# An attention and feed-forward kernel: eight more attention slots, spread over two feed-forward halves

## The chip, the cores and the metric

The kernel runs on one core of a Trainium2 chip. The metric is the device time of one execution in microseconds (us), as the median of several runs. Engines carry the profile's names: PE is the matrix engine and PEld its weight loads, DVE the vector engine, ACT the scalar engine, POOL GpSimd, and SP the engine that issues most DMAs.

## The reference

Causal attention with a decay bias, over 8 batches, 8 heads, 576 positions and 64 numbers a head, and behind it a feed-forward block on all 4608 tokens (512 to 2048 to 512, with a piecewise quadratic activation):

```python
scores = scale * np.matmul(q, k.transpose(0, 1, 3, 2))
cum = np.cumsum(np.maximum(s, 0.0), axis=-1)
bias = -(cum[:, :, :, None] - cum[:, :, None, :])
scores = np.where(causal, -1e9, scores + np.minimum(bias, 0.0))
attn = np.exp(scores - np.max(scores, axis=-1, keepdims=True))
attn = attn / (np.sum(attn, axis=-1, keepdims=True) + 1e-09)
x = np.matmul(attn, v)                  # heads laid side by side: tokens x 512
h = x @ w_in
g = np.where(h >= 1, h, np.where(h <= -1, 0.0, (h + 1) ** 2 / 4))
return g @ w_out
```

## The kernel before

**Attention jobs.** Two heads make a pair, so there are 32 pairs n (four to a batch b), and the 576 positions are cut into two halves: hf 0 holds positions 0 to 319 and hf 1 the other 256. A pair and a half make one of 64 jobs, in the order: for each batch, hf 0 of its four pairs, then hf 1 of its four pairs. A job is written as eight slots (`att_slot(j, k)`, k from 0 to 7). Slot 0 prepares the operands (`att_prep`: ACT casts Q1 in L325, K1 in L334 and Q2 in L335, DVE finishes Q1 in L336 and K2 in L339; each of these four tiles has one buffer, so the casts wait until the last scores of the job before are done). Slots 2 to 7 compute one unit of scores each: two PE matmuls (L384 with Q1 and K1, L385 with Q2 and K2) into a PSUM tile s, a minimum on DVE (L390), the exponential on ACT (L401). When both heads of a row block are there, `weights_t` scales them and splits them into pb (L422 to L425, L428), and a transposing DMA brings pb to pt (L429). Slot 7 also does `att_out` of the job before: the matmuls px from pt and vt (L447), and from px the feed-forward's input x (ACT in L458, DVE in L459). The tiles s and px share a ring of two PSUM buffers.

**Feed-forward halves.** Each batch and half is a feed-forward half of 16 steps (ft). Step ft computes a tile h from all four pairs of x (L501, 12 matmuls; the three of the last pair, kt 3, come last), then u and g on ACT, DVE and POOL (L513, L516, L517, L527, L528), and two steps later adds to four tiles y (L540, 12 matmuls). So a half is 384 matmuls, of 320 columns in hf 0 and of 256 in hf 1, and it needs the px of its batch's four jobs of the same hf. Its results leave through o (L554).

**The order.** One loop writes both down, job slots and feed-forward steps in turn. It has 512 rounds j. From round 32 on, a feed-forward half takes 32 rounds (step j // 2, h in even rounds and y in odd ones), and a round takes one attention slot, ahead of its feed-forward matmuls. In rounds 0 to 31, which hold the first half in an order of its own, every fourth round takes two slots:

```python
for _ in range(1 if j >= 2 * NFT else 1 + (j % 4 == 3)):
    att_slot(t // 8, t % 8)
    t += 1
```

The counter t starts at 32, as the first four jobs lie ahead of the loop. So feed-forward half number q starts, from q = 1 on, after slot 32q + 39, and slot 32q + 39 is the one that writes the px of the last job which that half needs. All 512 slots and the last px are written by round 480 of 512. The order in the source is a priority: the scheduler that builds the program places each instruction on its engine by that priority and by when it expects the inputs. On each engine, instructions then run strictly in the order placed.

Of the kernel before, what the change touches and what calls it, by code (L numbers as in the profile page):

```python
# [25 lines left out]
NFT = DFF // P  # L26
# [47 lines left out]
def attention_ffn(ctx: ExitStack, tc: tile.TileContext, qT, kT, vT, s, w_in, w_out, yT):  # L74
# [194 lines left out]
    def batch_scales(b):  # L269
        m = msc[b]  # L270
        h = hsc[b] = ap.tile([P, 1], F32, tag="hs", name=f"hs{b}")
        V.tensor_scalar(h, m, a_in, 2.0 ** -27, ALU.mult, ALU.mult)

        r = rsc[b] = ap.tile([P, 1], F32, tag="r", name=f"r{b}")
        i = r.bitcast(I32)
        V.tensor_scalar(r, m, a_in, 2048.0, ALU.mult, ALU.mult)
        V.tensor_scalar(r, r, 1.0, None, ALU.max)
        V.reciprocal(r, r)
        V.tensor_scalar(r, r, 2.0 ** 14, None, ALU.mult)
        V.tensor_scalar(i, i, 23, None, ALU.logical_shift_right)  # L280
        V.tensor_scalar(i, i, 127, None, ALU.add)
        V.tensor_scalar(i, i, 1, 23, ALU.logical_shift_right, ALU.logical_shift_left)

        u = usc[b] = ap.tile([P, 1], F32, tag="us", name=f"us{b}")
        V.tensor_scalar(u, h, r, None, ALU.mult)
        w = wsc[b] = ap.tile([P, 1], F32, tag="ws", name=f"ws{b}")
        V.tensor_scalar(w, u, 2.0, None, ALU.mult)
        c = ubi[b] = ap.tile([P, 1], F32, tag="ub", name=f"ub{b}")
        V.tensor_scalar(c, r, 0.5, None, ALU.mult)
        g = gsc[b] = ap.tile([P, 1], F32, tag="gb", name=f"gb{b}")  # L290
        V.reciprocal(g, r)
        V.tensor_scalar(g, g, g, 2.0 ** 14, ALU.mult, ALU.mult)

    def batch_y(b, groups=(0, 1)):
        ysc.setdefault(b, {})
        for i in groups:
            y = ysc[b][i] = ap.tile([P, 1], F32, tag=f"ys{i}", name=f"ys{b}_{i}")
            V.tensor_scalar(y, gsc[b], b_out[i], 2.0 ** -28, ALU.mult, ALU.mult)
# [168 lines left out]
    def att_slot(j, k):  # L467

        if j < len(jobs):
            n, hf = jobs[j]  # L470
            if k == 0:
                att_prep(n, hf)
            if k == 1 and hf == 0:
                v_prep(n)
            if k == V_K and hf == 0:
                v_turn(n)
            if k >= 2:
                scores(n, *UNITS[hf][k - 2])
            if k == 3 and j + 1 < len(jobs):
                att_load(*jobs[j + 1])  # L480
            if k == 1 and j % (2 * NPAIR) == V_J and j // (2 * NPAIR) + 1 < B:
                load_v(j // (2 * NPAIR) + 1)
            if k == 5 and j + 1 < len(jobs) and jobs[j + 1][0] % NPAIR == 0 and jobs[j + 1][1] == 0:
                with tc.issue_after(ttr[0]):
                    batch_start(jobs[j + 1][0] // NPAIR)
        if k == OUT_K and 1 <= j <= len(jobs) and j != NPAIR:
            while j == len(jobs) and late:
                late.pop(0)()
            att_out(*jobs[j - 1])
# [33 lines left out]
    def g_split(first=None):  # L523
        while to_split:
            g, u = to_split.pop()
            with tc.issue_after(first) if first is not None else ExitStack():
                A.copy(g[:, 0], u)  # L527
            G.tensor_tensor(g[:, 1], u, g[:, 0], ALU.subtract)  # L528
# [3 lines left out]
    def ffn_y(b, hf, ft, g, ms=tuple(range(NKT))):  # L532
        h_off, N, _ = HALF[hf]
        if ft == 0:
            for m in ms:
                ys[b, hf, m] = ps_y.tile([P, 512], F32, tag=f"y{m}", name=f"y{b}_{hf}_{m}")
        for m in ms:
            c0 = ft % 2 * 2 * P + m % 2 * P
            for n, (wl, gl) in enumerate(((0, 0), (1, 0), (0, 1))):
                T.matmul(  # L540
                    ys[b, hf, m][:, :N], WO[8 * (m // 2) + ft // 2][:, wl, c0:c0 + P], g[:, gl],
                    start=(ft == 0 and n == 0), stop=(ft == NFT - 1 and n == 2),
                )
        if ft == NFT - 1:
            last = (b, hf) == (B - 1, len(HALF) - 1)
            for m in ms:
                tag, bufs = ("u", 4) if last and m >= 2 else ("o", O_BUFS)
                o = gp.tile([P, N], F32, tag=tag, bufs=bufs, name=f"o{b}_{hf}_{m}")
                y = ys[b, hf, m][:, :N]
                with tc.high_priority(offset=FFN_LEAD):  # L550
                    if last and m % 2:
                        V.tensor_scalar(o, y, ysc[b][m // 2], None, ALU.mult)
                    else:
                        A.activation(o, y, AF.Copy, scale=ysc[b][m // 2])  # L554
                (nc.sync if last and m % 2 else nc.scalar).dma_start(
                    yT[m * P:(m + 1) * P, b * S + h_off:b * S + h_off + N], o
                )

    def ffn_step(s, k):

        b, hf, ft = s // (2 * NFT), s // NFT % 2, s % NFT
        if k == 0:
            ffn_q.append((b, hf, ft, ffn_h(b, hf, ft)))
        elif len(ffn_q) > Y_LAG:
            ffn_y(*ffn_q.pop(0))
# [39 lines left out]
    for j in range(16 * NP):  # L605
        if j % 64 == 48 and j // 64 + 1 < B:
            batch_scales(j // 64 + 1)
            batch_y(j // 64 + 1)
        for _ in range(1 if j >= 2 * NFT else 1 + (j % 4 == 3)):
            att_slot(t // 8, t % 8)  # L610
            t += 1
        with tc.high_priority(offset=W2_LEAD):
            for _ in range(W2_RATE):
                next(tasks, None)
        if j >= 2 * NFT:
            ffn_step(j // 2, j % 2)
        elif j < NFT:
            ffn_step(j, 0)
        else:
            if j == NFT:  # L620
                with tc.high_priority(offset=FFN_LEAD):
                    g_split()
            m = 2 * (j // 8 % 2)
            for i in range(j % 8 * 2, j % 8 * 2 + 2):
                ffn_y(*ffn_q[i], ms=(m, m + 1))
            if j == 2 * NFT - 1:
                del ffn_q[:NFT]
# [32 lines left out]
```

## Time and profile before

| | before |
|---|---|
| times of three runs | 1170.36, 1171.36 and 1180.07 us (median 1171.36) |
| profiled execution | 1178.29 us |
| its span, first to last instruction | 1176.2 us |
| granted PE clock, mean over the span | 0.967 |
| busy share of the span | PE 86%, PEld 66%, DVE 76%, ACT 63%, POOL 59% |
| DMA moved | 158.04 MB, mean 134 GB/s |

The profiled execution is one run, 0.6% above the median. Its share of busy time is an average over three stages: some 92 us ahead of the first feed-forward matmul, the long stage in which attention and feed-forward are mixed, and a last stretch with feed-forward work alone. The granted clock is 1.00 in most of the span and lower in a few places.

### The profile page before, as it was taken

The page shows a single profiled execution, that of the slowest core. Times are in us where ns is not written, and L with a number is a line of the kernel's source. Part 1 is how long each engine was busy: PE and PEld are TensorE (multiplying, and loading weights), DVE is VectorE, ACT ScalarE, POOL GpSimd, SP SyncE. Part 2 cuts the span into 40 slices and gives each one's busy share as a digit, 9 for nine tenths or more (in the row PEclk, how much of TensorE's full clock was granted, in tenths as well). Part 3 has the DMA queues.
Part 4 walks back from the last instruction along what each step waited for, and adds up shares of the span by engine and source line. Part 5 has one row for each costly group of instructions (what it writes and reads, how often), then busy time and mean ns, then how long its engine had stood idle before and what let it go on. Part 6 is the DMA issues. An engine that isn't in the chain of part 4 may idle for free.

```text
span 1176.2 us, 25135 instructions
## 1 busy us (share of the span) xinstructions
PE 1009.5 (86%) x8470; PEld 776.6 (66%) x8470; DVE 892.6 (76%) x2404; ACT 746.0 (63%) x1719; POOL 691.0 (59%) x1169
## 2 busy tenths in 40 slices
PE   0234678699999999799998999899989999899998
PEld 0122345487767867587767867677768867686787
DVE  6879998778777877768777777778778877787633
ACT  4656677567656765767557665667557764777533
POOL 3876268676556664656546654656557564675522
PEclk9997999799998999999999999899999999899999
DMA  8885536867637773776638672876547753767310
GB/s 243 206 195 138 165 85 145 159 139 153 130 73 180 147 148 74 166 139 144 131 84 168 152 149 65 173 142 156 119 98 172 153 133 75 163 132 157 74 34 19
DMA packets 343081, 158.04 MB, mean 134 GB/s; under 512 B 291112, under 2 KB 324264, under 8 KB 342952
## 3 DMA queue, kind: packets, MB, share of 16 engines
q1 hardware_dynamic: 333248, 146.50, 59.0%
q10 hardware_dynamic: 9704, 9.93, 2.7%
q8 instruction: 67, 1.10, 0.4%
q14 instruction: 62, 0.51, 0.1%
HBM read 75.33 MB, written 9.73 MB: 72 GB/s over the span
## 4 chain that ended last, share of the span: by engine, by line
PE 42%; DVE 8%; DMA 5%; POOL 5%; issue 3%; ACT 1%; DVEq 0%; ACTq 0%; POOLq 0%
PE y L540 18%; PE h L501 17%; DMA pt<-pb 4%; PE px L447 3%; POOL pb L422 2%; DVE pb L428 2%; PE s L384 2%; PE s L385 2%; DMA vt<-vb 2%; POOL pb L425 1%; DVE p L390 1%; DVE K L339 1%; DVE h L516 1%; DVE Q L336 1%; POOL vb L350 1%
## 5 line engine op out<-in xcount | busy, mean ns | idle before, releaser
L501 PE MATMUL h<-x,WI 128*128 128x256 f16 (+1 forms) x3072 | 453.0, 292 | 23.4 <-DVE u L517 21.0
L540 PE MATMUL y<-g,WO 128*128 128x256 f16 (+1 forms) x3072 | 453.2, 291 | 17.3 <-POOL g L528 7.4
L501 PEld LDWEIGHTS <-WI 128*128 128x128 f16 x3072 | 292.3, 100 | 118.2 <-issue 28.2
L540 PEld LDWEIGHTS <-WO 128*128 128x128 f16 x3072 | 287.1, 99 | 108.7 <-issue 19.3
L528 POOL TENSOR_TENSOR g<-u,g 128x320 f16<-128x320 f32 (+1 forms) x256 | 199.2, 778 | 209.1 <-ACT g L527 203.9
L513 ACT ACTIVATE u<-h,ub,us 128x320 f32<-128x320 f32 (+1 forms) x256 | 149.3, 584 | 171.8 <-PE h L501 146.7
L401 ACT ACTIVATE p<-p,mn 64x64 f32<-64x64 f32 (+4 forms) x320 | 178.8, 559 | 113.6 <-DVE mn L390 96.4
L516 DVE SCALAR_TENSOR_TENSOR h<-h,ws,u 128x320 f32<-128x320 f32 (+1 forms) x256 | 133.0, 520 | 118.4 <-ACT u L513 117.9
L422 POOL TENSOR_SCALAR pb<-p,rs 64x128 f16<-64x128 f32 (+4 forms) x160 | 113.7, 711 | 152.2 <-DVE rs L418 118.6
L384 PE MATMUL s<-K,Q 128*128 128x288 f32 (+4 forms) x384 | 150.9, 395 | 43.8 <-DVE mn L390 33.3
L428 DVE SCALAR_TENSOR_TENSOR pb<-p,rs,pb 64x128 f16<-64x128 f32 (+4 forms) x160 | 135.8, 849 | 52.0 <-POOL pb L422 51.6
L425 POOL TENSOR_TENSOR pb<-p,pb 64x128 f16<-64x128 f32 (+4 forms) x160 | 165.0, 1032 | 9.2
L390 DVE CUSTOM_DVE_ANT_0 p<-s,mask 64x64 f32<-64x64 f32 (+4 forms) x320 | 134.8, 422 | 41.1 <-PE s L385 36.7
L517 DVE SCALAR_TENSOR_TENSOR u<-u,r,h 128x320 f32<-128x320 f32 (+1 forms) x256 | 130.2, 510 | 7.5
L423 ACT ACTIVATE p<-p,rs 64x64 f32<-64x64 f32 (+4 forms) x160 | 89.3, 559 | 67.2 <-DVE rs L418 60.6
L385 PE MATMUL s<-K,Q 68*128 68x288 f32 (+4 forms) x384 | 121.8, 319 | 9.8 <-ACT p L423 5.5
L447 PE MATMUL px<-pt,vt 128*64 128x256 f16 (+3 forms) x1536 | 87.7, 260 | 38.0 <-DMA pt<-pb 21.8
L384 PEld LDWEIGHTS s<-K,Q 128*128 128x128 f32 (+1 forms) x384 | 74.3, 194 | 68.2 <-DVE mn L390 42.4
L527 ACT CAST g<-u 128x320 f16<-128x320 f32 (+1 forms) x256 | 108.1, 422 | 10.6 <-DVE u L517 10.6
L447 PEld LDWEIGHTS <-vt 128*64 128x64 f16 x1536 | 73.2, 113 | 61.5 <-issue 40.3
L424 POOL TENSOR_SCALAR pb<-p 64x128 f16<-64x128 f32 (+4 forms) x160 | 90.9, 569 | 6.0 <-ACT p L423 2.9
L385 PEld LDWEIGHTS s<-K,Q 68*128 68x128 f32 (+1 forms) x384 | 75.8, 198 | 12.2 <-ACT p L423 5.9
(116 smaller groups left out, 961.4 us busy)
## 6 DMA issues: line engine op xcount, KB each, us to landing
rk<-in_k_dram SPq DMA_DIRECT2D x64, 288.0 KB
rq<-in_q_dram SPq DMA_DIRECT2D x64, 160.0 KB
rk<-in_k_dram SPq DMA_DIRECT2D x64, 160.0 KB
v<-in_v_dram SPq DMA_DIRECT2D x32, 288.0 KB
wir<-in_moe_w_in_dram SPq DMA_DIRECT2D x16, 512.0 KB
rq<-in_q_dram SPq DMA_DIRECT2D x64, 128.0 KB
wor<-in_moe_w_out_dram SPq DMA_DIRECT2D x16, 512.0 KB
out_dram<-o ACTq DMA_DIRECT2D x32, 160.0 KB
```

The lines of the kernel that those rows point to most:

```text
L384: T.matmul(sc[:R, :c1 - c0], Q1[:, hd, qo:qo + R], K1[:, hd, c0:c1], start=True, stop=False)
L385: T.matmul(sc[:R, :c1 - c0], Q2[:KC, hd, qo:qo + R], K2[:KC, hd, c0:c1], start=False, stop=True)
L390: ttr[0] = V.tensor_tensor_reduce(out=Pt[:R, c0:c1], in0=sc[:R, :c1 - c0], in1=mask[:R, mo:mo + c1 - c0], scale=1.0, scalar=3.0e38 if mn i ...
L401: A.activation(Pt[:R, :W], Pt[:R, :W], AF.Exp, bias=m2[:R], scale=-1.0, accum_out=sums[n, i][:R, hd:hd + 1])
L425: G.tensor_tensor(los[1], pw, his[1], ALU.subtract)
L428: V.scalar_tensor_tensor(los[0], pv, rs[:R, :1], his[0], ALU.mult, ALU.subtract)
L447: T.matmul(px[hd * D:(hd + 1) * D, lo:N], VT[:, vl * NB + j, hd * D:(hd + 1) * D], PT[:, 4 * j + 2 * hd + pl, lo:], start=(m == 0), stop=( ...
L501: T.matmul(h[:, :N], WI[4 * kt + ft // 4][:, wl, ft % 4 * P:(ft % 4 + 1) * P], x[:, kt, xl], start=(n == 0), stop=(n == 3 * NKT - 1),)
L513: first = A.activation(u, h[:, :N], AF.Relu, bias=ubi[b], scale=usc[b]).ins
L516: V.scalar_tensor_tensor(h[:, :N], h[:, :N], wsc[b], u, ALU.mult, ALU.max)
L528: G.tensor_tensor(g[:, 1], u, g[:, 0], ALU.subtract)
L540: T.matmul(ys[b, hf, m][:, :N], WO[8 * (m // 2) + ft // 2][:, wl, c0:c0 + P], g[:, gl], start=(ft == 0 and n == 0), stop=(ft == NFT - 1 an ...
```

## The change

```diff
-        for _ in range(1 if j >= 2 * NFT else 1 + (j % 4 == 3)):
+        for _ in range(1 + (j % 4 == 3 if j < 2 * NFT else j % 8 == 3 and j < 6 * NFT)):
             att_slot(t // 8, t % 8)
             t += 1
```

NFT is 16. Rounds 0 to 31 are as before. In rounds 32 to 95 (the halves q = 1 and q = 2) every eighth round, from round 35 to round 91, takes a second slot: eight more. From round 96 on each slot stands eight rounds earlier beside the feed-forward than before, and the last slot is written by round 472. No instruction is added or taken away.

What that makes of the order on the engines, at the place where half hf 1 of batch 6 (q = 13) starts. On PE, px27_1 is the last px that this half needs (pair 27 is the last of batch 6), s28 and s29 are scores of the next jobs, h6_1_0 and h6_1_1 are the first two steps of the half, and y6_0_0 to y6_0_3 are the outputs of the half before. First the rows around the start of px27_1, before:

```order
L384 MATMUL s28_2_0_0_14171<-K1_90,Q1_89 128x320
L385 MATMUL s28_2_0_0_14171<-K2_92,Q2_91 128x320
L384 MATMUL s28_2_1_0_14200<-K1_90,Q1_89 128x320
L385 MATMUL s28_2_1_0_14200<-K2_92,Q2_91 128x320
L447 LDWEIGHTS vt27_12908
L447 MATMUL px27_1_14214<-pt27_1_13815,vt27_12908 64x256
```

And the rows ahead of the start of px27_1 in the changed kernel:

```order
L540 LDWEIGHTS WO15_139
L540 MATMUL y6_0_2_13514<-g6_0_12_14154,WO15_139 128x320
L540 LDWEIGHTS WO15_139
L540 MATMUL y6_0_3_13515<-g6_0_12_14154,WO15_139 128x320
L540 LDWEIGHTS WO15_139
L540 MATMUL y6_0_3_13515<-g6_0_12_14154,WO15_139 128x320
L447 LDWEIGHTS vt27_12760
L447 MATMUL px27_1_14089<-pt27_1_13690,vt27_12760 64x256
```

Before, px27_1 stood right behind the scores s28_2_1_0. Now 13 feed-forward matmuls (5 of h6_1_0 and 8 of y6_0) stand between them. From the last scores of px27_1's own job (s27_4_1_288) to px27_1 there were 58 feed-forward matmuls (40 of 320 columns and 18 of 256) and are now 93 (84 and 9); the scores and the other px in between are the same. For px28_1, the first hf 1 job of the next batch, the same count goes from 70 (42 and 28) to 104 (28 and 76).

Then the rows on PE behind the end of px27_1, before:

```order
L447 MATMUL px27_1_14214<-pt27_1_13815,vt27_12908 64x64
L384 MATMUL s29_0_0_0_14304<-K1_90,Q1_89 64x64
L385 MATMUL s29_0_0_0_14304<-K2_92,Q2_91 64x64
L501 LDWEIGHTS WI12_120
L501 MATMUL h6_1_0_14266<-x6_1_13487,WI12_120 128x256
L501 LDWEIGHTS WI12_120
L501 MATMUL h6_1_1_14312<-x6_1_13487,WI12_120 128x256
```

And in the changed kernel:

```order
L447 MATMUL px27_1_14089<-pt27_1_13690,vt27_12760 64x64
L384 MATMUL s29_0_0_0_14179<-K1_90,Q1_89 64x64
L540 LDWEIGHTS WO7_131
L540 MATMUL y6_0_0_13512<-g6_0_12_14154,WO7_131 128x320
L540 LDWEIGHTS WO7_131
L540 MATMUL y6_0_1_13513<-g6_0_12_14154,WO7_131 128x320
L385 MATMUL s29_0_0_0_14179<-K2_92,Q2_91 64x64
L540 LDWEIGHTS WO15_139
L540 MATMUL y6_0_2_13514<-g6_0_12_14154,WO15_139 128x320
L540 LDWEIGHTS WO15_139
L540 MATMUL y6_0_3_13515<-g6_0_12_14154,WO15_139 128x320
L501 LDWEIGHTS WI0_108
```

WI12 holds the weights of kt 3, so the first h matmul behind px27_1 was one that reads the x made from it. Now 13 others come first: four of y6_0 and the nine of h6_1_1 that read the three earlier pairs. Counted in feed-forward matmuls, px27_1 stood 6 behind the start of its half and stands 7 ahead of it; for the last px of an hf 0 half, 18 ahead become 63.

The third place is the preparation of job (30, hf 1), a little later, on ACT. Before:

```order
L325 ACTIVATE Q1_89<-rq30_1_15350 128x2x256
L332 DMA Q2_91<-cumd_106 2x2x256
L401 ACTIVATE p29_4_1_15431,sm29_4_15380<-p29_4_1_15431,mn29_4_1_288_15460 128x576
L333 DMA K2_92<-cumd_106 2x2x576
L334 CAST K1_90<-rk30_1_15351 128x1152
```

And in the changed kernel:

```order
L325 ACTIVATE Q1_89<-rq30_1_15225 128x2x256
L334 CAST K1_90<-rk30_1_15226 128x1152
L332 DMA Q2_91<-cumd_106 2x2x256
L333 DMA K2_92<-cumd_106 2x2x576
L554 ACTIVATE o6_1_0_15480<-y6_1_0_14550,ys6_0_12888 128x256
```

The cast of K1 now follows the cast of Q1 at once. On PE the distance that it has to cover shrinks: from the last scores of one job to the first scores of the next there stand, besides one px, 18 feed-forward matmuls in place of 25 for job (29, hf 1), 9 in place of 48 for (30, hf 1), and 10 in place of 36 for (31, hf 1).

## The prediction

> **What bounds the kernel now.** I read the page first, then stretches of the span, then PE's waits, and at last single rows at one of the places where PE waits.
>
> ```profile
> span 1176.2 us, 25135 instructions
> PE 1009.5 (86%) x8470; PEld 776.6 (66%) x8470; DVE 892.6 (76%) x2404; ACT 746.0 (63%) x1719; POOL 691.0 (59%) x1169
> PE   0234678699999999799998999899989999899998
> PEclk9997999799998999999999999899999999899999
> ```
>
> PE is the busiest engine, and from the eighth of 40 slices on it is at 9 tenths or nearly. Some slices of PE hold an 8 or a 7, and after the start PEclk falls in much the same places. So the mixed stage is bound by PE, except at places that recur. The stretches at six of these places, with one between two of them and one of the last stretch:
>
> ```profile
> core 0: us, PE busy (x) PEld busy (x) DVE busy (x) ACT busy (x) POOL busy (x), PEclk, DMA share, GB/s
> 352.00:365.00 13.00, 10.31 (x78) 7.80 (x77) 10.01 (x30) 9.13 (x25) 9.16 (x22) 0.74 0.92 209
> 482.00:504.00 22.00, 16.90 (x140) 13.04 (x136) 13.85 (x39) 14.58 (x39) 14.76 (x31) 0.84 0.86 192
> 614.00:635.00 21.00, 16.13 (x150) 13.07 (x151) 14.99 (x40) 15.46 (x42) 14.65 (x31) 0.92 1.00 181
> 744.00:765.00 21.00, 18.06 (x155) 14.31 (x156) 15.70 (x41) 15.54 (x42) 14.36 (x31) 0.84 0.89 181
> 876.00:892.00 16.00, 13.45 (x121) 10.12 (x122) 11.96 (x35) 11.90 (x35) 11.72 (x27) 0.89 0.97 208
> 1003.00:1016.00 13.00, 9.93 (x72) 7.41 (x73) 10.13 (x30) 10.31 (x28) 9.60 (x21) 0.74 0.89 162
> 1016.00:1072.00 56.00, 55.07 (x513) 45.97 (x510) 44.23 (x126) 39.42 (x102) 35.22 (x70) 1.00 0.67 145
> 1140.00:1170.00 30.00, 30.00 (x277) 26.89 (x276) 11.12 (x24) 9.44 (x22) 7.88 (x12) 1.00 0.01 1
> ```
>
> The last number but two is the granted clock. The places lie about 130 us apart ((1003 - 352) / 5), which is one batch, and each is where a half hf 1 starts. There the clock is 0.74 to 0.92, and in between 1.00, with PE busy 55.07 of 56 us. Clock lost is width times (1 - clock): 3.4, 3.5, 1.7, 3.4, 1.8 and 3.4 us. The last row gives the price of a feed-forward matmul where nothing is waited for: 30 us / 277 = 0.108 us at 256 columns, and I take 0.135 us (5/4 of it) at 320. What PE waits for, from the second of these places to the last px:
>
> ```profile
> engine line waited for: us in total, times, longest us
> PE px L447 <- DMA pt<-pb: 14.5, 11, 2.1
> PE s L384 <- DVE mn L390: 8.9, 10, 1.4
> PE y L540 <- POOL g L528: 7.1, 5, 2.6
> PE s L385 <- ACT p L423: 5.5, 5, 1.1
> PE px L447 <- DVE pb L428: 1.8, 1, 1.8
> ```
>
> Only waits of some length are listed; the first line is px waiting for the transposed weights, 11 times. One place in order of time on PE, where half q = 13 starts:
>
> ```profile
> 1001.75 0.42 PE L384 MATMUL s<-K,Q 128*128 128x320 f32 x1 [0.42 <-DVE mn L390]
> 1002.01 0.31 PE L385 MATMUL s<-K,Q 68*128 68x320 f32 x1
> 1003.70 1.51 PE L447 MATMUL px<-pt,vt 128*64 128x256 f16 x30 [1.38 <-DMA pt<-pb]
> 1005.14 0.24 PE L384 MATMUL s<-K,Q 128*64 128x64 f32 x1
> 1006.47 0.21 PE L385 MATMUL s<-K,Q 68*64 68x64 f32 x1 [1.09 <-ACT p L423]
> 1006.53 0.89 PE L501 MATMUL h<-x,WI 128*128 128x256 f16 x6
> ...
> 1009.08 0.53 PE L384 MATMUL s<-K,Q 128*128 128x192 f32 x1 [1.29 <-DVE mn L390]
> ...
> 1010.21 0.49 PE L540 MATMUL y<-g,WO 128*128 128x320 f16 x1
> ```
>
> From 1001.75 to 1010.21 there are only six h matmuls of feed-forward. The rest is a chain of the attention, with four waits: 0.42 + 1.38 + 1.09 + 1.29 = 4.2 us. The half cannot go on, since the x of its last pair is not there, and the matmuls ahead of it in PE's order are used up. The wait of 1.09 is put down to ACT, but L385 reads K2, and DVE ends that just ahead (1005.05 + 1.32), as it ends x at 1006.77:
>
> ```profile
> 1005.05 1.32 DVE L339 TENSOR_TENSOR K<-rk,K 64x640 fp32r<-64x640 f32 x1
> 1006.30 0.47 DVE L459 SCALAR_TENSOR_TENSOR x<-px,ex,x 128x256 f16<-128x256 f32 x1
> ```
>
> That the row of L385 reads 5.5 us in 5 times says that five such places are alike.
>
> **The change, part by part.** It removes and adds no instruction; it puts feed-forward matmuls where PE waited.
>
> *px at the start of hf 1.* From the last scores of its own job to px27_1 there was feed-forward work of 40 x 0.135 + 18 x 0.108 = 7.3 us, and there is 84 x 0.135 + 9 x 0.108 = 12.3 us now. 5.0 us more cover a wait of 1.38 us, and the 0.42 us ahead of it: both go. *K2 of the next job:* between s28_2_1_0 and its use in L385 come 10 matmuls at 0.135 and 5 at 0.108, 1.9 us, against waits of 1.38 + 1.09 = 2.5 us in the same interval; 0.6 us stay. *x:* from the end of px (1003.70 + 1.51) to the end of x it took 1.56 us, and 4 x 0.135 + 9 x 0.108 = 1.5 us now stand there where nothing stood: it just fits. *The scores behind it* (1.29 us): four h matmuls now stand ahead of s29_1_1_0, 0.4 us; 0.9 us stay. So 1.5 us of 4.2 us stay, and 2.7 us go, at five places (q = 5 to 13): **13.5 us**.
>
> *The clock at these five places.* It falls only where PE has such waits; what was lost is 3.5 + 1.7 + 3.4 + 1.8 + 3.4 = 13.8 us. Bounds are 0 and 13.8. With a third of the waits left I take three quarters: **10 us**. In the Trainium skill, "TensorE: Matmul & The Clock Gate", Part 1 and the table "Why this matters for your kernels" say that the clock halves after an idle window of about 3.4 us, and that gaps over about 3 us are to be avoided. The trace does not agree with a reading of that by single gaps, as no wait above is longer than 2.6 us; by that reading these stretches have another cause and this term would be 0.
>
> *px of the first hf 1 job* of each batch:
>
> ```profile
> 1070.45 0.29 PE L385 MATMUL s<-K,Q 68*128 68x288 f32 x1
> 1070.59 0.99 PE L540 MATMUL y<-g,WO 128*128 128x320 f16 x6
> 1072.80 0.41 PE L447 MATMUL px<-pt,vt 128*64 128x256 f16 x4 [1.21 <-DMA pt<-pb]
> ...
> 1056.00:1076.00 20.00, 18.68 (x163) 14.18 (x163) 16.52 (x41) 15.27 (x35) 11.93 (x19) 1.00 0.65 143
> ```
>
> Its feed-forward cover goes from 42 x 0.135 + 28 x 0.108 = 8.7 us to 28 x 0.135 + 76 x 0.108 = 12.0 us: 3.3 us more, against 1.21 us. Of the 14.5 us in the list, 5 x 1.4 are at the starts of hf 1; the other 7.5 and the 1.8 for pb are of this kind. I count **8 us**.
>
> *y waiting for g* (7.1 us in 5 times) comes from POOL and ACT being full of attention work around these places. Nothing in the order bounds it well: between 0 and 7.1 us; halfway, **3.5 us**. *The place at 352*, where only part of the lead is there: px gets cover, x none. Its clock cost 3.4 us and a px wait as at the others is 1.4 us; between 0 and some 7 us, taken: **2.5 us**.
>
> *The eight added slots* are one job. A batch takes 130 us, and its feed-forward 384 x (0.108 + 0.135) = 93 us, so a job costs PE up to (130 - 93) / 8 = 4.6 us. It moves from the last mixed rounds, where PE is full, to halves q = 1 and 2, where PE is nearly full as well: the sum is 0, with 4.6 us either way as the ends.
>
> *What is late next: the operands.* Behind px, less now stands between two jobs' scores. What the casts took, for jobs (29, hf 1) and (30, hf 1):
>
> ```profile
> 1059.10 0.30 PE L385 MATMUL s<-K,Q 68*128 68x288 f32 x1
> 1059.96 1.14 ACT L334 CAST K<-rk 128x1152 fp32r<-128x1152 f32 x1
> 1074.89 1.14 ACT L334 CAST K<-rk 128x1152 fp32r<-128x1152 f32 x1
> ```
>
> K1 is ready 1.7 us after the last scores (1059.40 to 1061.10) in the one, and 5.3 us (1070.74 to 1076.03) in the other. The cover falls to 9 or 10 matmuls, 1.1 to 1.3 us, and a px of up to 1.51 us: some 2.7 us. In the other case ACT had an exponential and an o between, because there was time; now K1 stands right behind Q1, which gives the 1.7 us. The ends are 0 and (5.3 - 2.7) = 2.6 us at three jobs in each of six batches, 47 us; nearest to the row with the same order on ACT, I take 0.7 us a batch: **4 us lost**. DMA moves the same bytes; SP issues the same transfers, moved along with their slots.
>
> The sum: 13.5 + 10 + 8 + 3.5 + 2.5 - 4 = 33.5 us. From the profiled execution's 1178.3 us that is 1144.8 us. It lies 6.9 us above the median of the runs, so I forecast 1171.4 - 33.5 = **1138 us**.
>
> **The rivals.** *The clock stays low at these places*, because the waits that are left are enough for it, or because it has another cause: 10 us less gain, 1148 us. For it: the clock falls where the longest single wait is 1.38 us. Against it: around 1072.80 a lone wait of 1.21 us leaves it at 1.00 (the last row above), so it is several waits close together that go with it. It is also the case that the gap rule of the Trainium skill's page on the clock gate would give. *The lead is not what the name says:* in feed-forward matmuls px27_1 moves by 13, not by the 96 that eight rounds hold, since the scheduler already placed attention by readiness. Then only the px waits go, 5 x 1.4 + 8 = 15 us, with 1 for the place at 352: 1155 us. Against it: px is not the only one with new cover. *No change:* waits move to other places, PE's order being as full as before: 1165 to 1175 us. *Slower:* the casts of the operands, as above. If K1 and Q1 end 5.3 us behind the last scores as they did at 1076.03, the 47 us are lost and 37.5 won, and each such wait of 2.6 us is as long as those that lowered the clock; with 1.7 us more (1.7 to 3.5 were lost at a place) at half of the 18, the time is 1171.4 + 9.5 + 15 = 1196 us. It decides from about 4.8 us: 18 x (4.8 - 2.7) = 37.8 us. The row that speaks against it is the cast at 1061.10. *More:* all bounds at the good end, 5 x 4.2 + 13.8 + 9.3 + 7.1 + 7 = 58 us, 1113 us.
>
> **How the numbers follow.** The forecast (1128 to 1146) gets 0.55, the clock 0.12, the short lead 0.12, more than forecast (1113 to 1128) 0.08, no change 0.08, slower 0.05. A measurement of this kernel can tell about 1% from no change, so faster means below 1159.7 us: 0.55 + 0.12 + 0.12 + 0.08 = 0.87; within 1% 0.08; slower 0.05. The range from 1120 to 1158 us leaves out the two last and about half of "more", some 0.17.
>
> **What would show it.** In the profile after: px waiting for pt falls from 11 times to three or fewer in the mixed stage; in each place where hf 1 starts y or h rows stand between s and px, and PE's clock there is 0.95 or more; L385 behind ACT p falls to 0.6 us a place; PE busy in these stretches is above 9 tenths. It would be wrong if L384 waits for Q or K more than 1 us a job (the casts), if the stretches of low clock stay in number, or if halves q = 1 and 2 take more than 5 us longer than the end wins back.

## The result: 3.4% less time, and the profile after

The changed kernel takes 1132.37 us (median of 4 runs, 1130.65 to 1136.65) where the kernel before takes 1170.92 us (4 runs on the same chip). The ratio measured over these runs is 0.9658, with a 95% interval from 0.9603 to 0.9714 (the two medians alone give 0.9671). The forecast was 1138 us, a gain of 33.5 us; the measured gain is 38.5 us. The profiled execution took 1131.28 us.

The same four lines of the page, now of the changed kernel:

```profile
span 1129.5 us, 25197 instructions
PE 988.2 (87%) x8470; PEld 770.9 (68%) x8470; DVE 879.3 (78%) x2404; ACT 740.2 (66%) x1719; POOL 682.4 (60%) x1169
PE   0234667799999999989998999999999999999998
PEclk9997899789999999999999999999999999999999
```

The work is the same (8470 matmuls; the 62 instructions more are semaphore events, that is, engines waiting for each other), but PE and its clock are at 9 tenths in nearly every slice from the ninth on. The stretches where the halves hf 1 start (q = 3 to 13), and one between:

```profile
341.00:355.00 14.00, 12.14 (x99) 8.97 (x97) 11.20 (x38) 9.63 (x30) 9.21 (x23) 0.88 0.91 187
470.00:490.00 20.00, 17.81 (x156) 14.51 (x152) 14.46 (x49) 14.69 (x43) 13.55 (x32) 0.91 0.85 181
595.00:611.00 16.00, 14.15 (x131) 11.79 (x131) 12.74 (x43) 13.44 (x40) 10.76 (x26) 1.00 0.96 203
717.00:733.00 16.00, 14.01 (x146) 11.73 (x140) 12.50 (x43) 13.01 (x39) 10.71 (x26) 1.00 1.04 214
838.00:854.00 16.00, 14.60 (x150) 12.24 (x147) 12.77 (x44) 13.53 (x39) 11.28 (x27) 1.00 1.02 216
961.00:977.00 16.00, 13.99 (x148) 11.82 (x143) 13.45 (x43) 13.20 (x38) 11.20 (x26) 1.00 0.77 178
977.00:1030.00 53.00, 52.19 (x493) 43.63 (x491) 42.82 (x115) 38.55 (x94) 33.84 (x66) 1.00 0.72 151
```

The clock lost there is 14 x 0.12 + 20 x 0.09 = 3.5 us; before it was 17.2 us. What PE waits for in the mixed stage, by the same view and over the same stretch as before:

```profile
PE s L384 <- DVE Q L336: 6.8, 6, 1.7
PE y L540 <- POOL g L528: 4.3, 5, 1.0
PE s L384 <- DVE mn L390: 3.8, 5, 1.0
PE px L447 <- DMA K<-cumd: 1.9, 2, 1.1
PE y L540 <- ACT g L527: 1.1, 5, 0.2
```

The first line of before (px waiting for pt, 14.5 us) is gone, as is L385 waiting behind ACT p. (Ahead of this stretch, at the place where q = 3 starts, one wait of 0.4 us for pt and one of 1.2 us behind ACT p are left.) A new line leads: scores waiting for Q from L336. The place where q = 13 starts, on PE:

```profile
958.74 0.31 PE L385 MATMUL s<-K,Q 68*128 68x320 f32 x1
958.89 0.72 PE L501 MATMUL h<-x,WI 128*128 128x256 f16 x5
959.45 1.25 PE L540 MATMUL y<-g,WO 128*128 128x320 f16 x8
960.63 1.51 PE L447 MATMUL px<-pt,vt 128*64 128x256 f16 x30
...
962.81 1.36 PE L501 MATMUL h<-x,WI 128*128 128x256 f16 x11
...
965.04 0.33 PE L384 MATMUL s<-K,Q 128*128 128x192 f32 x1 [0.78 <-DVE mn L390]
...
966.71 0.97 PE L540 MATMUL y<-g,WO 128*128 128x320 f16 x6 [0.22 <-ACT g L527]
```

The 13 feed-forward matmuls stand ahead of px, px starts without a wait, and 1.0 us of waiting is left of 4.2 us. At the four other places from q = 5 on, 0.5 to 1.4 us is left, counted in the same way.

In numbers, from the first h of half q = 3 to the end of the span: 831.7 us before (344.5 to 1176.2), 788.7 us after (340.8 to 1129.5), so 43.0 us less. All listed waits of PE from 340 us on fall from 44.2 to 20.4 us (23.8), the time at half clock from 34.1 to 6.8 us (half of the 27.3 us is 13.7), and a job of 4.6 us (an estimate) has gone to the halves before: 42.1 us. The two profiled executions differ by 47 us and the medians by 38.5 us, because the profiled run of before was one of its slower ones (its runs spread from 1170.4 to 1180.1); the split is that of the traces, its sum a little large.

### The profile page after: what moved, and what is told of

Its sections match the earlier page's. It is cut to its first block, busy times and chain, and to the rows that moved or that the text cites. A ratio compares the mean times of both kernels' runs of the same rounds, so it can differ in the third digit from the quotient of the medians.

```text
span 1129.5 us, 25197 instructions
## 1 busy us (share of the span) xinstructions
PE 988.2 (87%) x8470; PEld 770.9 (68%) x8470; DVE 879.3 (78%) x2404; ACT 740.2 (66%) x1719; POOL 682.4 (60%) x1169
## 4 chain that ended last, share of the span: by engine, by line
PE 58%; DVE 16%; POOL 7%; DMA 7%; issue 6%; ACT 5%; ACTq 0%; DVEq 0%; SPq 0%; POOLq 0%
PE y L540 24%; PE h L501 24%; PE px L447 4%; PE s L384 3%; PE s L385 3%; DVE pb L428 3%; DMA pt<-pb 3%; DVE p L390 2%; DVE Q L336 2%; POOL pb L422 2%; DVE h L516 1%; ACT p L401 1%; ACT u L513 1%; DMA wor<-in_moe_w_out_dram 1%; DVE u L517 1%
## 5 line engine op out<-in xcount | busy, mean ns | idle before, releaser
L501 PE MATMUL h<-x,WI 128*128 128x256 f16 (+1 forms) x3072 | 465.1, 291 | 25.6 <-DVE u L517 21.8
L528 POOL TENSOR_TENSOR g<-u,g 128x320 f16<-128x320 f32 (+1 forms) x256 | 203.9, 796 | 163.7 <-ACT g L527 162.8
L422 POOL TENSOR_SCALAR pb<-p,rs 64x128 f16<-64x128 f32 (+4 forms) x160 | 96.9, 606 | 163.1 <-DVE rs L418 111.1
L384 PE MATMUL s<-K,Q 128*128 128x288 f32 (+4 forms) x384 | 148.5, 388 | 44.5 <-DVE mn L390 25.1
L425 POOL TENSOR_TENSOR pb<-p,pb 64x128 f16<-64x128 f32 (+4 forms) x160 | 169.4, 1059 | 9.6
L385 PE MATMUL s<-K,Q 68*128 68x288 f32 (+4 forms) x384 | 121.3, 318 | 4.8 <-POOL K L339 3.6
L384 PEld LDWEIGHTS s<-K,Q 128*128 128x128 f32 (+1 forms) x384 | 73.2, 191 | 67.3 <-DVE mn L390 30.9
L447 PE MATMUL px<-pt,vt 128*64 128x256 f16 (+3 forms) x1536 | 82.8, 259 | 21.0 <-DVE mn L390 6.1
L424 POOL TENSOR_SCALAR pb<-p 64x128 f16<-64x128 f32 (+4 forms) x160 | 94.1, 588 | 10.6 <-ACT p L423 9.4
L385 PEld LDWEIGHTS s<-K,Q 68*128 68x128 f32 (+1 forms) x384 | 74.5, 195 | 8.0 <-POOL K L339 4.1
```

The lines of the kernel that those rows point to most:

```text
L384: T.matmul(sc[:R, :c1 - c0], Q1[:, hd, qo:qo + R], K1[:, hd, c0:c1], start=True, stop=False)
L385: T.matmul(sc[:R, :c1 - c0], Q2[:KC, hd, qo:qo + R], K2[:KC, hd, c0:c1], start=False, stop=True)
L425: G.tensor_tensor(los[1], pw, his[1], ALU.subtract)
L447: T.matmul(px[hd * D:(hd + 1) * D, lo:N], VT[:, vl * NB + j, hd * D:(hd + 1) * D], PT[:, 4 * j + 2 * hd + pl, lo:], start=(m == 0), stop=( ...
L501: T.matmul(h[:, :N], WI[4 * kt + ft // 4][:, wl, ft % 4 * P:(ft % 4 + 1) * P], x[:, kt, xl], start=(n == 0), stop=(n == 3 * NKT - 1),)
```

## The experiments

Theory: PE waited where a half hf 1 starts, because the chain px, x, operands and scores had no feed-forward work beside it; the change puts such work there, and the clock, which falls where PE has little to do, stays up with it. Rivals: the gain is the lead itself, counted in slots; it is made where the slots are added; the clock has a cause of its own. Each kernel's ratio is to the kernel before on the same chip; that kernel's median was 1170.9 us beside the changed kernel, 1175.4 us beside e1 to e4 and 1174.7 us beside e5 to e8. So rows are compared by their ratios.

| kernel | us | ratio (95% interval) |
|---|---|---|
| changed kernel | 1132.4 | 0.966 (0.960 to 0.971) |
| e1, two slots | 1145.8 | 0.975 (0.972 to 0.979) |
| e2, four slots | 1134.8 | 0.965 (0.961 to 0.969) |
| e3, eight slots, late | 1159.3 | 0.987 (0.983 to 0.991) |
| e4, before with fill | 1172.0 | 0.997 (0.995 to 1.000) |
| e5, two slots with fill | 1134.6 | 0.968 (0.964 to 0.971) |
| e6, slots in the first half | 1137.7 | 0.968 (0.966 to 0.971) |
| e7, changed, Q1 ahead of pb | 1136.7 | 0.966 (0.964 to 0.969) |
| e8, e6 and e7 together | 1137.3 | 0.969 (0.966 to 0.971) |

**e1 and e2: how much lead.**

```diff
-j % 8 == 3 and j < 6 * NFT     # the changed kernel: eight slots
+j % 16 == 3 and j < 4 * NFT    # e1: two
+j % 8 == 3 and j < 4 * NFT     # e2: four
```

> Two added slots in place of eight (rounds 35 and 51). By the order, PE then has as much feed-forward work ahead of the last px of a half hf 1 as would cover its wait (13.2 us of PE work from the job's last scores to px; 9.9 before the change, 14.9 with it), but none between that px and the h that reads its x (0.1 us; 0.1 and 1.6). Theory (each wait is covered by the work that stands in its way, and the clock falls with the waits that are left): the px waits go (about 15 us), K2, x and score waits stay at 2 to 3 us a place, the half-speed stretches stay or halve: 1145 to 1156 us. Rival (the gain is the lead in slots, 2 of 8): 38.5 x 2/8 = 10 us, 1161 us. Rival (any lead does it): 1132 us.

> Four added slots, in half q = 1 alone. From half q = 4 on the order on PE is then nearly that of eight slots (px to x and px cover the same numbers to 0.1 us), as the scheduler places attention when its inputs are ready and no longer by the lead. Theory (order and cover): 1132 us, within 4 us. Rival (one whole job of lead is what counts): half the gain, 1151 us.

Four slots give what eight give, and two give some 70% of it. Both times lie where the theory had them. So the lead in slots is not what counts; the cover in PE's order is: at the starts of hf 1 from q = 5 on, e2's trace has the same order of matmuls behind px as the changed kernel. In e1 PE waited, from 340 us to the start of the last half, for:

```profile
PE s L385 <- DMA K<-cumd: 10.1, 5, 3.0
PE s L384 <- DVE Q L336: 3.5, 6, 2.6
...
PE px L447 <- DMA pt<-pb: 0.7, 2, 0.4
```

px no longer waits for pt, as its cover said, and K2 does make PE wait, as nothing covers it there. At one of these places, at 727.47 us, DVE's part of K2 had ended at 725.96; the profile puts the end of that wait down to the transfer of rows into K2 (L333), which was issued at 724.32. Starting that transfer earlier was not tried. From 340 us to the last half e1 waits hardly more than the changed kernel (23.3 and 20.4 us); what it lacks is clock (34.1 against 6.8 us at half clock).

**e3: the same slots, later.**

```diff
-j % 8 == 3 and j < 6 * NFT
+j % 8 == 3 and 14 * NFT <= j < 18 * NFT
```

> The same eight slots, but in the halves q = 7 and 8 instead of 1 and 2. Up to half q = 7 the order is that of before, from q = 10 on that of the changed kernel. Theory (the gain is made at the start of each later half hf 1, and at each first px of hf 1): two places in full and one in part of the six, so 2 to 3 sixths of 38.5 us: 1152 to 1158 us, with px waits and half clock at the early places and none at the late ones in one and the same trace. Rival (the gain is made where the slots are added, in the thin first stage, or at the end): 1171 us or 1132 us.

The gain is 1.3%, about two fifths of the full one, as the theory had it; the time is 1 us above its range. The first line is the px wait up to 720 us; then come both stretches, with the granted clock next to last but two:

```profile
PE px L447 <- DMA pt<-pb: 6.4, 5, 1.8
...
340.00:720.00 380.00, 358.74 (x3085) 279.90 (x3084) 292.71 (x803) 250.16 (x605) 231.89 (x417) 0.97 0.67 139
720.00:1104.00 384.00, 373.60 (x3324) 294.45 (x3322) 297.25 (x837) 257.89 (x625) 235.37 (x423) 1.00 0.65 134
```

Up to 720 us px waits as before and the clock is 0.97; behind it there is no wait of px for pt, and the clock is 1.00. The gain is made at each later place and not where the slots are added.

**e4 and e5: the clock by itself.** Matmuls that nobody reads are put ahead of the px in question: 12 in the kernel before (e4), 20 in e1's kernel (e5).

```diff
+if p == 3 and hf == 1 and 4 < n < 31:
+    for _ in range(12):        # e5: 20
+        T.matmul(px[:, :N], WI[0][:, 0, :P], X[b, 0][:, 0, 0, :N], start=True, stop=True)
 for m, (j, vl, pl) in enumerate(steps):
```

> The kernel before, with 12 matmuls of 256 columns that nobody reads put ahead of the last px of hf 1 in batches 1 to 6 (into the px tile, which the first real px overwrites; the result does not change). They read old data, so they run while px waits for pt: the wait is filled, nothing else is covered. Theory (the clock falls because PE has little to do there): the wait stays as long as it was, 12 x 0.108 = 1.3 us of it are filled, the half-speed stretches get fewer or shorter, and the time falls by up to 10 us: 1160 to 1169 us. Rival (the low clock has another cause, and only waits count): 1171 to 1175 us with the clock as before.

> The kernel of e1 (two added slots), with 20 matmuls of 256 columns that nobody reads ahead of the last px of hf 1 in batches 1 to 6, 2.2 us each place. In e1 PE waits there for K2 of the next job (1.2 to 3.0 us), which is made meanwhile whatever PE does; so the idle time becomes matmuls without use, and no useful work is covered that was not before. Theory (the clock falls because PE has too little to do around these places; e1 lost some 14 us more to it than the changed kernel did, with waits of about the same total): the half-speed stretches go mostly, 1132 to 1140 us against 1145.8 us. Rival (the clock falls for another cause, and the waits are what counts): the clock as in e1, and 1145 to 1150 us.

e5 decides; its time lies in the theory's range. First four stretches of e1 around the starts of q = 7, 9, 11 and 13, then the same four places in e5:

```profile
595.00:615.00 20.00, 16.81 (x148) 13.21 (x146) 13.65 (x44) 14.36 (x40) 12.43 (x28) 0.83 0.87 172
720.00:740.00 20.00, 17.74 (x149) 13.75 (x147) 14.93 (x45) 14.88 (x41) 13.01 (x29) 0.83 0.81 176
850.00:870.00 20.00, 17.49 (x159) 13.56 (x157) 15.07 (x44) 15.99 (x42) 13.40 (x29) 0.91 0.86 176
973.00:993.00 20.00, 17.75 (x149) 13.49 (x147) 15.39 (x47) 15.89 (x43) 12.85 (x30) 0.83 0.67 144
```

```profile
587.00:607.00 20.00, 18.41 (x181) 14.90 (x179) 14.69 (x49) 16.14 (x45) 12.99 (x30) 1.00 1.02 206
710.00:730.00 20.00, 17.43 (x161) 14.11 (x160) 13.19 (x43) 14.20 (x38) 11.67 (x27) 0.91 0.95 180
834.00:854.00 20.00, 17.10 (x166) 13.72 (x165) 13.30 (x44) 15.45 (x41) 11.55 (x27) 0.98 0.97 199
960.00:980.00 20.00, 18.14 (x169) 14.78 (x167) 14.19 (x48) 15.03 (x40) 12.25 (x28) 0.91 0.81 158
```

Over all six places e1 lost 13.8 us of clock and e5 4.0 us. From 340 us to the last half, with the stretches at half clock outside these windows (at 513 and 769 us in e1, and most of one at 853 us in e5), it is 17.1 and 5.1 us. The 120 added matmuls cost 120 x 0.108 = 13 us, PE's listed waits fell by 9.9 us (23.3 to 13.4), and the time fell by 0.75% (0.9751 to 0.9676), 9 us: 17.1 - 5.1 + 9.9 - 13 = 8.9 us. The waits alone would have made e5 3 us slower. PE's busy time over the whole span says the same, e1 first:

```profile
PE 1004.3 (88%) x8470; PEld 777.8 (68%) x8470; DVE 890.3 (78%) x2404; ACT 745.9 (65%) x1719; POOL 690.7 (60%) x1169
PE 1001.9 (88%) x8590; PEld 782.7 (69%) x8590; DVE 878.5 (78%) x2404; ACT 744.0 (66%) x1719; POOL 679.2 (60%) x1169
```

With 120 matmuls more, PE is busy for 2.4 us less. So work without use, put where PE had nothing to do, made the kernel faster, and it did so by the clock. One thing besides the filler differs: the scheduler placed some matmuls in another order (behind px, for instance, four h matmuls stand together where e1 has two and two), and what that alone is worth was not measured.

e4 points the same way but weakly: 3.4 us of gain, with the clock still low (0.72 to 0.91) at five of the six places, because waits other than the filled one stay there. Its time lies in the range of the rival, but its clock does not stay as it was: the time at half clock behind 340 us falls from 34.1 to 20.5 us. Of its expectation only the direction came true.

**e6, e7 and e8: can more be had?** e6 adds the slots in the first half; e7 swaps two instructions on DVE; e8 does both.

```diff
-1 + (j % 4 == 3 if j < 2 * NFT else j % 8 == 3 and j < 6 * NFT)
+1 + (j % 2 == 1 and j < 2 * NFT)                    # e6, e8
```

```diff
-V.scalar_tensor_tensor(Q1[D:, :, :N], ...)          # L336; e7, e8:
+q1 = V.scalar_tensor_tensor(Q1[D:, :, :N], ...).ins
+if held(n, hf):                                     # hf 0, the last pair of a batch from 1 on
+    with tc.issue_after(q1):
+        late.pop(0)()                               # L428 of the job before
...
-if late:                                            # in scores()
+if late and not (i == 2 and held(n + 1, 0)):
```

> The eight slots in rounds 0 to 31 (two slots in every second round) and not in halves 1 and 2. By the order the start of half q = 3 is then covered as the later ones are. Theory (each engine's own bound in each stage): some 3 us less at q = 3 (1.2 us of wait and 1.7 us of clock), 4.6 us of a job's PE work taken from the stage that PE bounds; but rounds 0 to 31 are bound by DVE (83 to 85 us busy of 92), and a job is 62 / 8 = 7.8 us of DVE, so the first stage grows by about as much: 1129 to 1136 us, with the first hf 1 half 5 to 8 us later. Rival (PE is half idle in the first stage, so that attention is free there): 1125 us or less.

> The changed kernel, and at the last hf 0 job of each batch from 1 on DVE's part of Q1 (L336) is issued ahead of one pb (L428), which waits for POOL. The two stand the other way round in the changed kernel, where PE waits 6.8 us in 6 times for Q1. Theory (that wait is DVE's order alone): it goes, 4 to 7 us less, 1125 to 1129 us where the changed kernel has 1132 us. Rival (pb then comes later and the wait moves to px or to the scores behind): no change, within 2 us.

> e6 and e7 together. Theory: the two effects add up, so e7's time plus what e6 shows against the changed kernel: 1122 to 1130 us. Rival: 1132 us, as one place of waits is traded for another.

e6 is the changed kernel's equal, 2 us above its expected range and far from its rival's. The first row is the changed kernel up to its half q = 2, the second e6:

```profile
90.00:278.00 188.00, 140.26 (x1066) 102.13 (x1067) 163.21 (x409) 132.56 (x274) 119.06 (x168) 0.88 0.60 140
90.00:287.00 197.00, 144.54 (x1068) 104.37 (x1067) 163.53 (x411) 132.66 (x277) 119.72 (x171) 0.87 0.58 137
```

The same number of matmuls takes 9 us longer there, at the same DVE load; from the start of q = 2 to the end e6 is about 2 us faster (851.1 us in the changed kernel, 849.2 us in e6), less than was worked out. So PE's idle time in the first stage was not free for attention. But the reason that was expected, a first stage made longer by DVE, is not what the traces show: the first half hf 1 starts when it did (180.8 us in e6, 180.9 us in the changed kernel), and from there to the start of q = 2 PE is idle for 21.5 us in place of 13.0 us while DVE is busy for 80.1 and 79.1 us. Why PE waits longer there stays open. For e7, the wait that it was aimed at, in the changed kernel on PE and then on DVE:

```profile
620.08 0.21 PE L384 MATMUL s<-K,Q 128*64 128x64 f32 x1 [1.16 <-DVE Q L336]
...
618.12 0.61 DVE L428 SCALAR_TENSOR_TENSOR pb<-p,rs,pb 128x256 f16<-128x256 f32 x1 [1.94 <-POOL pb L422]
618.76 1.18 DVE L336 SCALAR_TENSOR_TENSOR Q<-rq,Q 64x640 fp32r<-64x640 f32 x1
```

DVE stands 1.94 us before pb with Q1 queued behind it, and PE waits for Q1. With Q1 first that line is gone from e7's waits, but others grew:

```profile
PE y L546 <- POOL g L534: 5.9, 9, 1.0
PE s L390 <- DVE mn L396: 4.6, 6, 1.3
PE px L453 <- DMA pt<-pb: 1.9, 4, 0.9
```

All listed waits from 340 us on fall by 3.1 us only (20.4 to 17.3), and in these two traces the time at half clock grows from 6.8 to 13.7 us, which costs 3.4 us. The time is the same: the rival holds, and the 4 to 7 us of the theory did not come. e8 does not add two effects up either; the rival holds there too (0.969, where 0.966 is the changed kernel's). Nothing tried beats the changed kernel.

## Why the prediction was right, by its steps

- **px, x, K2 and scores at the start of hf 1** (13.5 us): right, rather too small. At q = 13 1.0 us stays of 4.2 us, where 1.5 us was worked out; over the five places 5 us stay of 21 us, so some 16 us went. e1 shows the parts: px's cover alone takes px's wait away, and K2's wait stays until it has cover of its own. That K2 was late by DVE's part (L339) is not settled: in e1 it was the transfer of L333 that ended last.
- **The clock** (10 us of 13.8): the five places lose 1.8 us where they lost 13.8 us, so some 12 us went. It was the least certain term, and the rival on it fell with e5.
- **px of the first hf 1 job** (8 us): the waits for pt and pb (9.3 us) are gone. 2.5 us of other waits (1.9 and 0.6) came up ahead of three px of hf 0 (at 397, 645 and 889 us), so some 7 us over all px.
- **y waiting for g** (3.5 us): 7.1 to 4.3 us, 2.8 us.
- **The place at 352** (2.5 us): too small. Its clock lost is 1.7 us after and 3.4 us before, and of its waits (4.5 us) 1.2 us stay: 5.0 us.
- **The added slots** (0, with 4.6 us either way): the halves q = 1 and 2 did not grow. From the first h of q = 1 to that of q = 3 it takes 159.9 us where it took 162.4 us, with a job more in it: at the good end. So the 4.6 us (an estimate) that the job took out of the later halves were won, where the sum has 0.
- **The operands** (4 us lost): the size was near (6.8 us) and the step wrong. The casts on ACT were in time, as the row at 1061.10 had said; late was DVE's share of Q1, behind a pb that waits for POOL, at the last hf 0 job. That queue was not looked at.
- **The signs.** px waiting for pt and L385 behind ACT p went as forecast. The clock reached 0.95 at four of the six places (0.88 and 0.91 at the others), and PE is busy for 0.87 to 0.91 of these stretches, not above 9 tenths. L384 waits for Q 1.1 us at a time, in one job of eight, so the sign for late operands came true in part.
- **The sum.** The terms were worked out from one trace and gave 33.5 us; the traces differ by 43.0 us from q = 3 on, the medians by 38.5 us. The mechanism is as forecast; the places at hf 1, the clock and the added slots were sized too small, and so was the loss at the operands. That the median is met within 6 us is in part luck, since the trace of before was 7 us longer than its median.
- **The rival of the short lead** had the fact right (13 matmuls, not 96) and the conclusion wrong: e2 shows that the lead saturates, and that the little that is placed is enough.

## What to carry to other kernels

Where an engine is the bound, list its waits by place and not by kind: here one place in each batch held most of the gain. Count what the placed order puts between a producer and its use against the time that the trace shows for that chain, since the lead written in the source says little where a scheduler places by readiness. A wait of a microsecond on PE may cost twice, once as a wait and once as clock behind it.

## What the runs showed of the hardware

Behind 340 us the granted clock fell to half for stretches of 3.4 or 6.8 us without any long gap: in e1 around 727 us the longest single wait of PE was 1.99 us, and in the kernel before 1.38 us at 1003 us. Between the waits PE ran small matmuls. By the Trainium skill ("TensorE: Matmul & The Clock Gate", "Why this matters for your kernels") a gap of about 3 us is what to avoid; here several shorter ones within some 7 us had the same effect, and matmuls without use in their place took most of it away (e5).

The clock records of the ten traces show more. In each trace the clock changes only at times that are whole multiples of 3.41 us apart, wherever the work stands. Cut into these windows, the place at q = 13 in the kernel before, and then in the changed kernel, reads:

```profile
1005.32:1008.73 3.41, 1.38 (x12) 1.05 (x11) 2.40 (x5) 2.81 (x8) 2.59 (x7) 1.00 0.81 116
1008.74:1015.56 6.82, 6.49 (x26) 4.39 (x27) 5.46 (x20) 4.92 (x15) 4.76 (x11) 0.50 1.01 198
961.57:964.98 3.41, 2.69 (x37) 2.17 (x31) 1.81 (x9) 1.38 (x5) 2.86 (x6) 1.00 0.82 200
```

Before, PE is busy for 1.38 us of one window (0.40), and the next two are at half clock; in the changed kernel the lowest window there has 2.69 us (0.79), and the clock stays. Between 330 us and 55 us before the end, the ten traces hold 2174 such windows at full clock. The next window was at half clock behind all 13 in which PE was busy for less than 0.42, behind 24 of the 52 between 0.42 and 0.60, behind 2 of the 13 between 0.60 and 0.65, and behind 1 of the 2096 above. So what counted here was the busy share of a fixed window, not the longest gap. Where the waits fall in the windows decides part of the loss: in the kernel before, the starts of q = 7, 9, 11 and 13 have the same four waits, 4.2 or 4.3 us at each, and are followed by one, two, one and two windows at half clock. These are counts of these traces; PE's busy times in them are partly modelled, and no run was made to find a limit.
